# A fused retention and hard-swish MoE kernel: seven input buffers instead of six, and other places for transposes and attention steps between the matmuls

## The chip, the core and the metric

The kernel runs on one core of one Trainium2 chip. A core has five engines with a queue of instructions each: TensorE (PE: matmuls; PEld is its weight load), VectorE (DVE), ScalarE (ACT), GpSimd (POOL) and SyncE (SP), and 16 DMA engines that all queues share. The metric is the device time of one execution in microseconds (us), as the median of several runs. A profile is one further execution with a trace.

## What is computed

Retention (attention with a decaying causal mask and no softmax) for 8 batches and 8 heads, 576 positions, head size 64; its output, put together over the heads, goes through two matrix products with a hard-swish between them:

```python
scores = scale * np.matmul(q, k.transpose(0, 1, 3, 2))
ret = scores * Dmat[None, :, :, :]        # gamma[h] ** (i - j) for i >= j, else 0
attn = np.matmul(ret, v)
x = attn.transpose(0, 2, 1, 3).reshape(4608, 512)
h = x @ w_in                              # 512 -> 2048
g = h * np.clip(h + 3.0, 0.0, 6.0) / 6.0
out = g @ w_out                           # 2048 -> 512
```

## The kernel before

**Pieces.** The sequence of each batch is cut into four main pieces of 128 positions and a rest of 64; two rests make one "rest" piece. That gives 36 pieces, numbered 0 to 35 in the order of work; 12, 21, 30 and 35 are rest pieces. Within a batch a state (the decayed sum of k times v) is carried from one main piece to the next; a rest piece ends a batch and updates no state.

**Blocks.** The 4,608 tokens form nine blocks of 512: block b has the four main pieces of batch b, block 8 all the rests. For each block GEMM1 (`g1`, L539, 16 groups of four matmuls, then a Relu on ACT at L546 and a gate `gt` on DVE at L547) is followed by GEMM2 (`g2`, L597, 16 units of four matmuls: four token groups with four parts each; the last part copies the output to SBUF at L601 and stores it from SP at L582). GEMM1 of a block needs the outputs `xt16` of its four pieces.

**What lies between the matmuls.** Attention of later pieces is put between the units of GEMM2, by a list written by hand: `steps_at[block][j]` names what comes behind unit j (-1: ahead of the first), and `put` (L782 on) runs it. A step ends one pair of pieces and begins the next: `step` for pairs 8/9 and 10/11, `step4` from pair 12/13 on. `step4` multiplies the ended pair's queries with the carried state (L444), makes the scores of the begun pair (L411) and its state updates (L497), then the ended pair's attention times v (L465) and its copies to `xt16`. On DVE it does the state sums (L513, L528, L529) and the mask (L417). A tiny copy on ACT (`seen`, L456) reads the end of the first products, and the ended pair's last matmuls wait for it.

**What a piece needs ahead of its step.** `load` (L85) issues three DMAs from POOL (kn, q and v; six half-size ones for a rest piece), which also convert to 16 bit. `ahead` issues a DMA transpose of k from SP (`transpose_k`, L289), a scaling of q and v on DVE (`transpose_q`, L294), and a DMA transpose of the scaled q from SP (L295). `ahead_at[block][j]` says behind which unit. Pieces 0 to 7 are transposed on PE instead.

**Queues and buffers.** Every queue works in order, so that an instruction that waits holds what is behind it. Loaded pieces lie in `NBUF` = 6 buffers of kn and of qv. A buffer is taken by a later piece when its state update has read kn, its k is transposed, and its q and v are scaled; `load_until` only sets the place in the program, and as POOL issues nothing but these loads in this part, it is the waits that set their time. A buffer that is given back first is taken first. `step4` calls `load_until` for its last begun piece plus NBUF.

**Holds.** A manual dependency keeps loads 12 and later back until q of piece 10 is scaled (`transpose_q_and_load`, L701).

**Places that the change touches:** `NBUF` (L83), `update_mm` (L346 on), `first_step` (L669 on), `transpose_q_and_load`, and the tables from L826 on.

Of the kernel before, what the change touches and what calls it, by code (L numbers as in the profile page):

```python
# [17 lines left out]
def kernel(  # L18
# [16 lines left out]
    nc = tc.nc  # L35
# [4 lines left out]
    NPAIR = H // 2  # L40
# [14 lines left out]
    for b in range(B):  # L55
# [3 lines left out]
        if b >= 2 and b % 2 == 0 or b == B - 1:  # L59
            j = (b - 1) // 2  # L60
# [19 lines left out]

    loaded = {}
    EARLY = 4
    NBUF = 6  # L83

    def load(c):  # L85
        kn = nat.tile([P, H, D], FP16, tag="kn", bufs=NBUF, name=f"kn_{c}")
        qv = nat.tile([P, 2, H, D], FP16, tag="qv", bufs=NBUF, name=f"qv_{c}")
        loaded[c] = {"kn": kn, "qv": qv, "q16": qv[:, 0], "dma": []}
        for dst, src in ((kn, k), (qv[:, 0], q), (qv[:, 1], v)):
            for p0, b, s0, n in pieces[c][3]:  # L90
                loaded[c]["dma"].append(nc.gpsimd.dma_start(  # L91
                    dst[p0:p0 + n], src[b, :, s0:s0 + n, :].rearrange("h s d -> s h d")))
# [22 lines left out]
    first = const.tile([P, 1], FP32)  # L115
# [81 lines left out]
    def run_later(n):  # L197
        for _ in range(n):
            if later:
                later.pop(0)()  # L200
# [128 lines left out]
    def intra(c, copy_later=False, more=False):  # L329
        o, at, vs = st[c]["o"], st[c]["at"], st[c]["vs"]  # L330
        for p in range(NPAIR):
            for h2 in range(2):
                r = slice(h2 * HALF, h2 * HALF + HALF)
                nc.tensor.matmul(o[r, p, :], vs[:, 2 * p + h2, :], at[:, h2, p, :],  # L334
                                 start=(st[c]["first"] and p == 0),
                                 stop=(p == NPAIR - 1 and not more), skip_group_check=True)
        g0 = column_of(c)

        def copy():
            nc.scalar.copy(xt16[:, :, g0:g0 + P], o)  # L340

        if copy_later:
            return copy
        copy()

    def update_mm(cs):  # L346

        if not cs:
            return
        u = psum.tile([P, len(cs), NPAIR, D], FP32, tag="tu", name=f"u_{cs[0]}")  # L350
        for j, c in enumerate(cs):
            kn, vs = loaded[c]["kn"], st[c]["vs"]
            st[c]["u"] = u[:, j]
            for p in range(NPAIR):
                for h2 in range(2):
                    r = slice(h2 * HALF, h2 * HALF + HALF)
                    nc.tensor.matmul(u[r, j, p, :], kn[:, 2 * p + h2, :], vs[:, 2 * p + h2, :],
                                     start=(j == 0 and p == 0),
                                     stop=(j == len(cs) - 1 and p == NPAIR - 1),
                                     skip_group_check=True)  # L360

    def update_state(c, copies_later=False):
        kind, b, i, _ = pieces[c]
        last = i == PER - 1
        u = st[c]["u"]
        scale = gc_b[1 if i == PER - 1 and b % 2 else 0]
        ts = work.tile([P, NPAIR, D], FP16, tag="te" if last else "ts", bufs=4, name=f"ts_{c}")
        if i == 0:
            nc.vector.tensor_tensor(out=ts, in0=u, in1=scale, op=ALU.mult)
        else:  # L370
            ta = work.tile([P, NPAIR, D], FP32, tag="ta", bufs=2, name=f"ta_{c}")
            nc.vector.tensor_tensor(out=ta, in0=u, in1=st[c - 1]["ts"], op=ALU.add)
            nc.vector.tensor_tensor(out=ts, in0=ta, in1=scale, op=ALU.mult)
        st[c]["ts"] = ts
        old = state_of.get(b)
        if last:

            state_of[b] = None
            ts_of[b] = lambda h2, p: ts[rows(h2), p, :]
        else:  # L380
            new = free_tbd.pop(0)
            state_of[b] = new
        if old is not None and st[c].get("o") is not None:
            free_tbd.append(old)
        elif old is not None:
            st[c]["before"] = old
            st[c]["last_reader"] = True

        def copies():
            nc.scalar.copy(tbd[new][0:HALF, :, 0:D], ts[0:HALF])  # L390
            nc.scalar.copy(tbd[new][HALF:P, :, D:2 * D], ts[HALF:P])

        if last:
            return
        if copies_later:
            later.append(copies)
        else:
            copies()
# [192 lines left out]
    def g2(kb, mc, part):  # L591
        gt = gts[kb]
        if part == 0:
            pouts[kb, mc] = psum.tile([P, DM], FP32, tag="ph", bufs=4, name=f"pout_{kb}_{mc}")
        pout = pouts[kb, mc]
        for fc in range(4 * part, 4 * part + 4):
            nc.tensor.matmul(pout, gt[:, fc, P * mc:P * mc + P], wout16[:, fc, :],  # L597
                             start=(fc == 0), stop=(fc == NFC - 1))
        if part == 3:
            osb = work.tile([P, DM], FP32, tag="osb", bufs=4, name=f"osb_{kb}_{mc}")  # L600
            nc.scalar.copy(osb, pout)  # L601
            store(kb, mc, slice(0, DM), osb)
# [55 lines left out]
    def load_until(c):  # L658
        while next_load[0] < NP and next_load[0] <= c:
            load(next_load[0])  # L660
            next_load[0] += 1
# [4 lines left out]
    def unit2(kb, mc, part):  # L666
        return lambda: g2(kb, mc, part)

    def first_step(c):  # L669


        old, new, b = c - 1 >= EARLY, c + 1 < 8, pieces[c - 1][1]
        if old:
            before = state_of.get(b)
            tag, bufs = ("ph", 4) if c == 6 else ("o", 1)
            o = psum.tile([P, NPAIR, P], FP32, tag=tag, bufs=bufs, name=f"o_{c - 1}")
            st[c - 1].update(o=o, first=True)
            copy = intra(c - 1, copy_later=True, more=before is not None)
            update_mm([c - 1])
            load_until(min(c - 1 + NBUF, 11))  # L680
            update_state(c - 1, copies_later=True)
        if new:
            q_by_pe(c + 1)
        if old and new:
            run_later(9)
        if EARLY <= c < 8:
            scores(c, 0)
        if old and before is not None:
            for p in range(NPAIR):
                nc.tensor.matmul(o[:, p, :], tbd[before][:, p, :], st[c - 1]["qk"][:, 0, p, :],  # L690
                                 start=False, stop=(p == NPAIR - 1), skip_group_check=True)
        if new:
            k_by_pe(c + 1, "ph" if old else "tu")
        if old:
            copy()
        if c < 8:
            run_later(9)
        if EARLY <= c < 8:
            scale_v(c)

    def transpose_q_and_load(c):  # L701

        scaled = transpose_q(c)
        load_until(7 + NBUF)
        tc.add_manual_dep(
            loaded[12]["dma"][0].ins, scaled.ins.name,
            mybir.DependencyInfo(mybir.DependencyClass.Sync, mybir.DependencyReason.DATA),
            reason="transposes of block 2 first")

    def ahead(c):  # L710
        transpose_k(c)
# [22 lines left out]
    def step(ended, begun):  # L734
# [10 lines left out]
        for c in begun:  # L745
            load_until(c + NBUF)
            run_later(1)
# [5 lines left out]
    def step4(ended, begun):  # L753
# [5 lines left out]
        if ended:  # L759
            inter_done(ended)  # L760
            intra4(ended)
            outputs4(ended)
        load_until(begun[-1] + NBUF)
        for c in begun[:-1]:
# [52 lines left out]
    for fc, cols in ((2, done), (0, last), (1, last), (3, done), (2, last), (3, last)):  # L817
# [7 lines left out]

    pairs = [[c, c + 1] for c in range(8, NP, 2)]  # L826
    steps_at = {1: {-1: [(step, [], pairs[0])], 7: [(step, pairs[0], pairs[1])],
                    12: [(step, pairs[1], [])], 15: [(load_until, 18)]},
                2: {-1: [(step4, [], pairs[2])]}}
    i = 2  # L830
    for kb, at in ((2, (4, 8, 13)), (3, (4, 12)), (4, (4, 12)), (5, (4, 12)), (6, (2, 6))):
        for j in at:
            steps_at.setdefault(kb, {})[j] = [(step4, pairs[i], pairs[i + 1])]
            i += 1
    steps_at[6][10] = [(inter4, pairs[i]), (inter_done, pairs[i])]
    steps_at[6][11] = [(end4, pairs[i])]

    ahead_at = {1: {10: 12, 11: 13, 13: 14, 14: 15, 15: 16}, 2: {0: 17, 2: 18, 7: 19, 14: 20, 15: 21},
                3: {0: 22, 1: 23, 13: 24, 14: 25}, 4: {0: 26, 1: 27, 13: 28, 14: 29},
                5: {0: 30, 1: 31, 12: 32, 13: 33, 14: 34, 15: 35}}  # L840
    for kb in range(1, NMB - 1):
        steps = steps_at.get(kb, {})
        for j, c in ahead_at.get(kb, {}).items():
            steps.setdefault(j, []).append((ahead, c))
        put([unit2(kb, mc, part) for mc in range(MBLK // P) for part in range(4)], steps)
        gts.pop(kb)
        gemm1(kb + 1, {})
# [34 lines left out]
```

## Time and profile before

| What | Value |
|---|---|
| Median of 3 runs | 310.26 us (310.15 to 310.31) |
| Profiled execution | 311.19 us |
| Its span, first to last instruction | 309.4 us |
| Mean granted TensorE clock | 0.989 |
| GEMM1 matmuls, L539 (128x512) | 560 in the trace, 123.3 us busy |
| GEMM2 matmuls, L597 (128x512) | 560 in the trace, 127.5 us busy |
| Scalings of q and v, L294 | 28, mean 685 ns |
| Gates, L547 | 144, mean 687 ns |
| DMA transposes of k and of q, to landing | 28 each, median 4.5 and 4.6 us |
| Loads of kn, q, v (128 KB), to landing | 32 each, median 5.6, 5.6 and 6.8 us |

Busy time of an engine is the union of its instructions. Waits are put down to the event that ended last before the waiting instruction began. The time outside the span is 311.19 - 309.4 = 1.8 us. "Landing" runs from the start of a DMA's issue to its completion. In the timelines each row begins with its start and its length in us, and brackets hold the idle time of the engine before it and what ended it.

### The profile page before, as it was taken

Reading aid. Unit: us, or ns where it says so; the run is one execution under the profiler, and the core shown is the slowest. Engines: PE = TensorE matmul, PEld = TensorE weight load, DVE = VectorE, ACT = ScalarE, POOL = GpSimd, SP = SyncE. Lnnn points to the kernel's source line nnn. Section 1 sums busy time; section 2 is a strip of 40 time slices with the busy share of each in tenths; the row PEclk is TensorE's granted clock in tenths of the full one; section 3 lists DMA queues with packets and bytes.
Section 4 is the critical chain, followed back from the end, with each engine's and each line's share of the span. In section 5 each row is a group of like instructions: output and inputs, shape, how many; then the busy total and the mean of one; then the engine's idle time right before and its main releaser. Section 6 shows DMA issues by size and latency. Waiting matters only on the chain.

```text
span 309.4 us, 7338 instructions
## 1 busy us (share of the span) xinstructions
PE 296.9 (96%) x3035; PEld 148.0 (48%) x3035; DVE 179.2 (58%) x307; ACT 167.2 (54%) x302; POOL 107.7 (35%) x134
## 2 busy tenths in 40 slices
PE   6999999999999986999999999999999999999994
PEld 2654455545544543445544554455445544444443
DVE  4768437895768753775097519754886337207700
ACT  5468447764378342673367436743774457227611
POOL 8963587086900686333240275323000000000000
PEclk9999999999999996899999999999999999999999
DMA  9999999999997999999992999899330110010022
GB/s 70 151 201 202 190 157 210 159 142 152 182 194 110 91 179 170 150 115 75 168 137 69 53 188 142 108 95 171 68 90 15 57 70 0 34 70 34 1 68 68
DMA packets 153169, 35.60 MB, mean 115 GB/s; under 512 B 143792, under 2 KB 148656, under 8 KB 153136
## 3 DMA queue, kind: packets, MB, share of 16 engines
q0 software_dynamic: 117264, 18.36, 91.2%
q1 hardware_dynamic: 35472, 16.26, 29.4%
q8 instruction: 23, 0.38, 0.5%
q10 hardware_dynamic: 400, 0.52, 0.5%
q14 instruction: 10, 0.08, 0.1%
HBM read 36.70 MB, written 9.44 MB: 149 GB/s over the span
## 4 chain that ended last, share of the span: by engine, by line
PE 79%; DMA 8%; issue 6%; DVE 3%; POOL 2%; ACT 1%; POOLq 0%; DVEq 0%
PE ph L539 33%; PE pout L597 33%; DMA qk<-vs 3%; DMA qv<-in_q_dram 3%; DMA qk<-kn 2%; PE o L444 2%; PE ph L562 1%; POOL kn L91 1%; PE pout L610 1%; PE o L465 1%; PE o L334 1%; PE sc L305 1%; PE sc L411 1%; PE trq L227 1%; PE u L497 1%
## 5 line engine op out<-in xcount | busy, mean ns | idle before, releaser
L597 PE MATMUL pout<-wout,gt 128*128 128x512 f16 x560 | 127.5, 383 | 0.0
L547 DVE SCALAR_TENSOR_TENSOR gt<-u,ph 128x512 f16<-128x512 f32 x144 | 97.4, 687 | 47.5 <-ACT u L546 47.1
L539 PE MATMUL ph<-xt,win 128*128 128x512 f16 x560 | 123.3, 380 | 1.0 <-DVE gt L547 1.0
L546 ACT ACTIVATE u<-ph,cb 128x512 f32<-128x512 f32 x144 | 98.4, 687 | 26.8 <-PE ph L539 24.7
L539 PEld LDWEIGHTS <-win 128*128 128x128 f16 x560 | 54.9, 98 | 67.8 <-issue 2.9
L597 PEld LDWEIGHTS <-gt 128*128 128x128 f16 x560 | 53.5, 98 | 62.6 <-issue 1.6
L91 POOL DMA_DIRECT2D kn<-in_k_dram x40 | 34.6, 867 | 92.9 <-PE u L497 56.8
L601 ACT COPY osb<-pout 128x512 f32<-128x512 f32 x35 | 20.5, 586 | 58.8 <-PE pout L597 57.9
L91 POOL DMA_DIRECT2D qv<-in_q_dram x40 | 34.6, 870 | 4.5 <-DMA wout<-in_moe_w_out_dram 3.1
L91 POOL DMA_DIRECT2D qv<-in_v_dram x40 | 34.8, 877 | 2.0 <-DMA wout<-in_moe_w_out_dram 1.7
L294 DVE TENSOR_TENSOR vs<-qv,gqv 128x1024 f16<-128x1024 f16 x28 | 18.1, 685 | 2.0 <-DMA qv<-in_q_dram 2.0
L309 DVE TENSOR_TENSOR at<-sc,mask_wide 128x1024 f16<-128x1024 f32 x9 | 11.0, 1222 | 13.9 <-PE sc L305 13.8
L513 DVE TENSOR_TENSOR th<-u,ts 128x256 f32<-128x256 f32 x15 | 6.4, 425 | 21.1 <-PE u L497 20.7
L528 DVE TENSOR_TENSOR ta<-u,th 128x256 f32<-128x256 f32 x20 | 8.4, 420 | 15.9 <-ACT th L516 15.1
L417 DVE TENSOR_TENSOR at<-sc,mask 128x1024 f16<-128x1024 f32 x12 | 14.6, 1217 | 4.4 <-PE sc L411 4.4
L475 ACT CAST xt<-o 128x512 f16<-128x512 f32 x16 | 8.6, 589 | 9.6 <-PE o L465 9.6
L456 ACT COPY seen<-o 128x1 f32<-128x1 f32 x12 | 1.9, 160 | 15.9 <-PE o L444 15.9
L518 ACT CAST tm<-th 128x256 f16<-128x256 f32 x20 | 8.2, 412 | 2.5 <-DVE th L513 1.9
L411 PE MATMUL sc<-qk 64*64 64x64 f16 x384 | 6.3, 197 | 3.1 <-DMA qk<-vs 3.1
L529 DVE TENSOR_TENSOR ts<-ta,gc 128x256 f16<-128x256 f32 x20 | 8.5, 425 | 0.7
L340 ACT CAST xt<-o 128x512 f16<-128x512 f32 x11 | 6.3, 589 | 3.5 <-PE o L690 1.7
L219 ACT COPY qk<-trk 128x512 f16<-128x512 f16 x8 | 4.7, 587 | 4.9 <-PE trk L218 4.8
(89 smaller groups left out, 159.5 us busy)
## 6 DMA issues: line engine op xcount, KB each, us to landing
out_dram<-osb SPq DMA_DIRECT2D x32, 256.0 KB, 4.3
kn<-in_k_dram POOLq DMA_DIRECT2D x32, 128.0 KB, 5.6
qv<-in_q_dram POOLq DMA_DIRECT2D x32, 128.0 KB, 5.6
qv<-in_v_dram POOLq DMA_DIRECT2D x32, 128.0 KB, 6.8
wout<-in_moe_w_out_dram POOLq DMA_DIRECT2D x4, 512.0 KB, 15.2
win<-in_moe_w_in_dram POOLq DMA_DIRECT2D x3, 512.0 KB, 8.0
win<-in_moe_w_in_dram POOLq DMA_DIRECT2D x2, 256.0 KB, 5.6
kn<-in_k_dram POOLq DMA_DIRECT2D x8, 64.0 KB, 4.1
```

What stands on the lines that cost most here:

```text
L91: loaded[c]["dma"].append(nc.gpsimd.dma_start(dst[p0:p0 + n], src[b, :, s0:s0 + n, :].rearrange("h s d -> s h d")))
L294: scaled = nc.vector.tensor_tensor(out=vs, in0=loaded[c]["qv"], in1=gqv, op=ALU.mult)
L309: later.append(lambda: nc.vector.tensor_tensor(out=at.rearrange("t a b s -> t (a b) s"), in0=sc.rearrange("t a b s -> t (a b) s"), in1=mas ...
L411: nc.tensor.matmul(sc[rows(half), h2, j, p, :], qk[rows(h2), 1, p, rows(half)], qk[rows(h2), 0, p, rows(half)], start=True, stop=True)
L417: nc.vector.tensor_tensor(out=at.rearrange("t a j p s -> t (a j p) s"), in0=sc.rearrange("t a j p s -> t (a j p) s"), in1=mask64[:, None, ...
L475: nc.scalar.copy(xt16[:, :, g0:g0 + 2 * P].rearrange("e p (j x s) -> e p j x s", j=2, x=2) [:, :, :, half, :], o[half].rearrange("e j p s ...
L529: nc.vector.tensor_tensor(out=ts, in0=ta, in1=scale, op=ALU.mult)
L539: nc.tensor.matmul(ph, win16[:, dmc, P * fc:P * fc + P], xt16[:, dmc, t0:t0 + MBLK], start=(dmc == 0), stop=(dmc == NCC - 1))
L546: nc.scalar.activation(u, ph, ACTF.Relu, bias=cb[:, 0:1], scale=1.0 / 6.0)
L547: nc.vector.scalar_tensor_tensor(out=gts[kb][:, fc, :], in0=u, scalar=1.0, in1=ph, op0=ALU.min, op1=ALU.mult)
L597: nc.tensor.matmul(pout, gt[:, fc, P * mc:P * mc + P], wout16[:, fc, :], start=(fc == 0), stop=(fc == NFC - 1))
L601: nc.scalar.copy(osb, pout)
```

## The change

`NBUF` becomes 7. `update_mm` returns its last matmul, and the manual dependency gets a helper, `hold`: loads 10 and 11 are held to the state updates of pieces 4 and 5, load 12 to the scaling of piece 10.

```diff
-    NBUF = 6
+    NBUF = 7
...
+    def hold(c, after):
+        tc.add_manual_dep(
+            loaded[c]["dma"][0].ins, after.ins.name,
+            mybir.DependencyInfo(mybir.DependencyClass.Sync, mybir.DependencyReason.DATA),
+            reason="what is wanted sooner has the queues")
...
-            update_mm([c - 1])
-            load_until(min(c - 1 + NBUF, 11))
+            added = update_mm([c - 1])
+            load_until(min(c + 5, 11))
+            if c + 5 in (10, 11):
+                hold(c + 5, added)
...
-        load_until(7 + NBUF)
-        tc.add_manual_dep(
-            loaded[12]["dma"][0].ins, scaled.ins.name,
-            mybir.DependencyInfo(mybir.DependencyClass.Sync, mybir.DependencyReason.DATA),
-            reason="transposes of block 2 first")
+        load_until(13)
+        hold(12, scaled)
```

The tables get other places. Steps in GEMM2 of block 2 stand behind units 3, 7 and 12 instead of 4, 8 and 13; in blocks 3 to 5 the second step stands behind unit 11 instead of 12; in block 6 the second step and the end of the last pair move two units back.

```diff
-                    12: [(step, pairs[1], [])], 15: [(load_until, 18)]},
+                    12: [(step, pairs[1], [])]},
...
-    for kb, at in ((2, (4, 8, 13)), (3, (4, 12)), (4, (4, 12)), (5, (4, 12)), (6, (2, 6))):
+    for kb, at in ((2, (3, 7, 12)), (3, (4, 11)), (4, (4, 11)), (5, (4, 11)), (6, (2, 8))):
...
-    steps_at[6][10] = [(inter4, pairs[i]), (inter_done, pairs[i])]
-    steps_at[6][11] = [(end4, pairs[i])]
-
-    ahead_at = {1: {10: 12, 11: 13, 13: 14, 14: 15, 15: 16}, 2: {0: 17, 2: 18, 7: 19, 14: 20, 15: 21},
-                3: {0: 22, 1: 23, 13: 24, 14: 25}, 4: {0: 26, 1: 27, 13: 28, 14: 29},
-                5: {0: 30, 1: 31, 12: 32, 13: 33, 14: 34, 15: 35}}
+    steps_at[6][12] = [(inter4, pairs[i]), (inter_done, pairs[i])]
+    steps_at[6][13] = [(end4, pairs[i])]
+
+    ahead_at = {1: {10: (12,), 11: (13,), 13: (14,), 14: (15,), 15: (16, 17)},
+                2: {1: (18,), 3: (19,), 9: (20,), 10: (21,)}, 3: {0: (22,), 1: (23,), 7: (24,), 8: (25,)},
+                4: {0: (26,), 1: (27,), 7: (28,), 8: (29,)}, 5: {0: (30,), 1: (31,), 7: (32,), 8: (33,)},
+                6: {0: (34,), 1: (35,)}}
```

`ahead` of a piece that stands behind the same unit as a step comes after that step. With these lists the scaling and the transposes of 17 move ahead of GEMM1 of block 2, those of 18 to 21 to earlier units of block 2, those of 24, 25, 28, 29, 32 and 33 from the end of a GEMM2 to its middle, and those of 34 and 35 into block 6.

## The prediction

> **What bounds the kernel now.** I read the page first, then the waits of PE, its timeline around the one visible hole, the chain back from there, and last the queues behind it.
>
> ```profile
> PE 296.9 (96%) x3035; PEld 148.0 (48%) x3035; DVE 179.2 (58%) x307; ACT 167.2 (54%) x302; POOL 107.7 (35%) x134
> PEclk9999999999999996899999999999999999999999
> ```
>
> PE is busy for 96% of the span, so it sets the time; only its holes, and the slices with a lower clock, can be won. The clock digit falls at slices 15 and 16 (116 to 131 us), and nowhere else.
>
> ```profile
> PE sc L411 <- DMA qk<-vs: 3.1, 1, 3.1
> ...
> PE ph L539 <- DVE gt L547: 1.0, 2, 0.6
> PE o L444 <- issue: 0.8, 1, 0.8
> ```
>
> These three are all of PE's waits after 51 us. The columns are total us, times, longest. The first and third are one place:
>
> ```profile
> 114.98 0.19 PE L444 MATMUL o<-qk,ts 64*64 64x64 f16 x1
> 115.98 0.28 PE L444 MATMUL o<-qk,ts 64*64 64x64 f16 x7 [0.81 <-issue]
> ...
> 116.21 0.31 PE L411 MATMUL sc<-qk 64*64 64x64 f16 x14
> 119.58 0.43 PE L411 MATMUL sc<-qk 64*64 64x64 f16 x16 [3.06 <-DMA qk<-vs]
> ```
>
> This is the attention step that begins pieces 18 and 19, inside GEMM2 of block 2. The scores of 19 wait for its transposed q. The stretch after the wait runs at half clock (columns: PE, PEld, DVE, ACT, POOL busy, granted clock, DMA, GB/s):
>
> ```profile
> 118.50:125.40 6.90, 5.83 (x91) 2.79 (x91) 4.66 (x9) 2.37 (x5) 4.40 (x6) 0.51 2.18 172
> ```
>
> Why the transposed q is late, from the chain, then SP's and POOL's queues:
>
> ```profile
> 110.87 8.67 DMA qk<-vs
> ```
> ```profile
> 103.02 1.19 SPq L295 DMA_TRANSPOSE qk<-vs  x1
> 104.32 1.21 SPq L289 DMA_TRANSPOSE qk<-kn  x1
> ...
> 109.09 1.68 SPq L289 DMA_TRANSPOSE qk<-kn  x1
> 110.87 1.72 SPq L295 DMA_TRANSPOSE qk<-vs  x1
> ```
> ```profile
> 82.45 0.93 POOL L91 DMA_DIRECT2D kn<-in_k_dram  x1
> ...
> 99.91 0.88 POOL L91 DMA_DIRECT2D kn<-in_k_dram  x1 [14.78 <-PE u L497]
> ...
> 105.18 0.88 POOL L91 DMA_DIRECT2D kn<-in_k_dram  x1 [2.64 <-PE u L497]
> ```
>
> The transposition of q19 is issued at 110.87 and takes 8.67 us to land, where the page's median for this kind is 4.6. It is issued late because its scaling on DVE stands at 108.85, and lands late because loads 20 and 21 (issued 105.18 to 111.9) are in the same DMA engines. POOL idles 14.78 us before load 19 (99.91): six buffers, and the next becomes free only with the state update of piece 13.
>
> The DVE wait of PE is at 159.68 and 191.04. Before the first:
>
> ```profile
> 157.75 1.29 DVE L294 TENSOR_TENSOR vs<-qv,gqv 128x1024 f16<-128x1024 f16 x2
> 158.95 3.20 DVE L547 SCALAR_TENSOR_TENSOR gt<-u,ph 128x512 f16<-128x512 f32 x5
> ```
>
> Two scalings of 0.64 us stand behind the step's state work and ahead of GEMM1's first gates; five gates then run without a gap, PE having filled its banks.
>
> **The change, part by part.** No instruction is added or removed; order and waits move.
>
> *Seven buffers.* Loads to 15 keep their times: 10 and 11 are held by the same updates as now, 12 by the same scaling, and POOL does not idle at 14. Load 16 need not wait for update 10 (POOL's 2.60 us idle at 77.25): it goes at 74.6; 17 and 18 at 77.25 and 79.85. Load 19 takes the buffer of 12, a rest piece that has no state update, and asks only for 12's transposition, which load 18 already meets at 82.45. So 19 is issued at 82.45, not 99.91, and 20 at 99.91, not 105.18.
>
> *Transposes sooner, steps one unit earlier.* A unit of GEMM2 is four matmuls, 4.42/5 = 0.88 us (99.46 to 103.88 holds five). The new walk: 99.46 + 4 x 0.88 = 103.00, step 14/15 (103.88 to 105.24: 1.36) to 104.36, four units (3.56) to 107.92, step 16/17 (108.80 to 110.41: 1.61) to 109.53, five units to 113.95, step 18/19 (as these two, 1.5) to 115.45, three units to 118.10. GEMM1 of block 3 then begins at 118.10, now at 124.18: 6.08 us. It takes 14.41 us now (to 138.59) against 13.90 for the one of block 2 (85.05 to 98.95): 0.51 more. Together 6.6. Cross-check: holes 0.81 + 3.06, and half of 119.58 to 125.40 (2.91), are 6.8. I take 6.6.
>
> *Is q19 there in time?* Step 18/19 wants it some 0.65 us in, at 114.6. Its scaling follows the DVE work of step 14/15, which ends 0.88 earlier than now (108.92): scaled at 108.7, issued then. With the median 4.6 it lands at 113.3, with today's 8.67 at 117.4: 0 to 2.8 us of hole. Which? By work: up to its landing at 119.54 the engines now also carry load 19 (3 x 0.87, POOL's spacing), two transposes (of 17 and 18; 1.30 each, SP's spacing at 103.02 and 104.32) and a store (estimate 1.4, what is left of 99.91 to 119.54 after nine loads and five transposes, with some 2.5 us of start), 6.6 us that move away; 1 to 1.5 of it does not fit into the lull of 95 to 101 us and stays. 119.54 - 6.6 + 1.2 = 114.1: in time by 0.5. I take 0.2.
>
> The row says that a transposition waits out the loads issued ahead of it. The Trainium skill ("DMA: Bandwidth & Descriptors", section on queues, rings and completion order) says that each DMA engine goes round between the queues packet by packet; by that q19 would share from its issue and land near 113, and the 0.2 would fall away. Landing 8.67 against 4.6 speaks for the row.
>
> *Scaling of 17 moves ahead of GEMM1 of block 2.* DVE works in order: behind it stand that GEMM1's gates, and PE waits for these when four banks are full (fifth group at 85.05 + 4 x 0.864 = 88.5). Now the scaling of 16 ends a 1.98 us wait at 84.47, for a v issued at 78.99: 5.5 us. Load 17 has that slot, with three loads (2.6) more in front: it lands at 84.5 to 87.1. From 87.1, scaling and first gate (0.69 each) end at 88.5. 0 to 0.1 us; up to 0.9 if 17 gains nothing. I take 0.2.
>
> *Scalings of 20 and 21* go in front of step 18/19's state work, wanted at about 115.3. Load 21 goes 104.3 to 108.4; the page's medians of 4.7 (half loads) to 6.8 give 113.1 to 115.2, scaled by 115.9 at worst. State work (120.46 to 124.32: 3.9) ends by 119.8; the first gate is wanted at 118.10 + 1.84 = 119.9. Nothing, with 1.6 us of banks behind it.
>
> *Later blocks:* second step behind unit 11, scalings at units 7 and 8. The state work of 182.88's step ends 6.3 us after its start, the first gate is wanted at 1.7 + 4 x 0.88 + 1.84 = 7.0. The 1.0 us of PE's DVE waits goes. The copy of unit 11's output (0.59) now stands on ACT ahead of the small copy that releases the step's last matmuls; it ends some 0.8 us into the step, they begin at 0.9: nothing, or 0.1 in each of five steps without that cover. On SP the stores stand behind more transposes; four output buffers cover that. Transposes 22/23 to 30/31 keep some 2.5 us to their steps (now 3.4). In block 6 the last step ends two units before GEMM1 of block 7 instead of four; its two copies (0.37 + 0.39) end 0.9 us ahead of it: nothing.
>
> **Sum.** 6.6 + 1.0 - 0.2 - 0.2 = 7.2. Span 309.4 - 7.2 = 302.2; the profiled execution takes 311.19, 1.8 outside its span: 304.0. It is 0.93 above the median of the plain runs (310.26), so the median should read 303.1.
>
> **The rivals.**
>
> 1. *q19 is still late.* Landing 8.67 after its issue gives a hole of 2.8 us. For: the engines are full from 104 us on either way. Against: 6.6 us of work is gone from in front. The hole alone gives 310.26 - 7.6 + 2.8 = 305.5; with the half clock that set in 2.3 us after PE ran dry (116.2 to 118.5) and lasted 6.8, some 3.1 more: 308.6. The Trainium skill ("TensorE: Matmul & The Clock Gate", Part 1) puts the drop behind an idle window of 3.4 us that runs freely; by that a hole of 2.8 may go without it, and 305.5 would stand. The row dropped sooner.
>
> 2. *Load 19 doesn't move*, because its buffer is not free at 82.45. For: on POOL it stands behind every earlier load, and any of them that waits holds it. Against: load 18 meets the very same transposition today without idling. Then only the DVE waits go: 309.3.
>
> 3. *Slower: DVE held by piece 17.* One instruction, the scaling of 17, with all gates of GEMM1 of block 2 behind it. PE's hole is landing + 0.69 + 0.69 + 0.1 - 88.5 = landing - 87.0, and beyond 2.3 us the half clock adds about 2.9. It eats the 7.6 when 17 lands after 91.7, 4.6 us later than I expect. For: 70 to 80 us has the busiest DMA of the trace (2.8 of 5 us), and load 16 adds to it. Against: the v that is issued in this slot now lands by 84.47. A landing at 94 gives 310.26 - 7.6 + 7.0 + 2.9 = 312.6.
>
> **How the numbers follow.** No new hole, 302 to 304.3: 0.72. Rival 1, 304.3 to 308.6: 0.14. Rival 2: 0.05. Rival 3, slower: 0.09. The time is that of the first, 303.1. The range begins at 301.9: 310.26 - 7.6 with neither 0.2 taken is 302.7, the cross-check's 6.8 gives 302.5, and 0.6 is left for PE's small waits on issue ahead of weight loads (4.3 us in nine places at L444), of which a less crowded DMA may spare some. It ends at 306.5, in the midst of rival 1. A change within 0.2% (0.6 us) can't be told from none: faster 0.88, same 0.03, slower 0.09.
>
> **What would show it.** Right: clock 1.00 throughout after 51 us, no DMA wait of PE, POOL's load at 82 followed by one more without the 14.78 us idle, no scalings directly ahead of gates in blocks 3 and 4. Wrong: PE waiting at L411 (L412 in the new numbering) near 114 us (rival 1), a DVE wait for qv near 86 us with PE waiting for a gate at 88.5 (rival 3), or POOL idle to 99.9 before load 19 (rival 2).

## The result, and the profile after

| What | Before | After |
|---|---|---|
| Median of the runs side by side | 310.28 us (310.15 to 311.26) | 307.17 us (307.02 to 307.6) |
| Profiled execution | 311.19 us | 307.60 us |
| Its span | 309.4 us | 305.8 us |
| Mean granted TensorE clock | 0.989 | 0.987 |
| Loads of v, to landing | 6.8 us | 8.2 us |

The changed kernel takes 0.9895 of the time before (95% interval 0.9873 to 0.9918): 3.1 us less, where 7.2 were forecast, and 0.7 us above the end of the forecast range (306.5). Ratios, here and below, leave out executions that were over 1.5% longer than the fastest of their kernel, while medians and ranges hold all of them, so that a ratio isn't the quotient of two medians. What the change was to remove is gone; two other waits stand in its place. First the page of the changed kernel: PE's share, and the clock in 40 slices.

```profile
PE 294.1 (96%) x3035; PEld 146.6 (48%) x3035; DVE 179.7 (59%) x307; ACT 167.7 (55%) x302; POOL 107.9 (35%) x134
PEclk9599999999999999999999999999999999999999
```

The dip at slices 15 and 16 has gone; there is one at the start instead, where before had none. PE's waits after 60 us (total us, times, longest):

```profile
PE ph L540 <- DVE gt L548: 2.0, 1, 2.0
PE ph L540 <- issue: 1.0, 1, 1.0
PE sc L412 <- DMA qk<-vs: 0.2, 1, 0.2
```

The 3.1 us for the transposed q of 19 (L411, now L412) are 0.2, and the two gate waits of before (at 159.68 and 191.04) are gone. New are one gate wait of 2.0 and an "issue" of 1.0, at these places of PE's timeline:

```profile
85.65 3.62 PE L540 MATMUL ph<-xt,win 128*128 128x512 f16 x16
91.22 10.52 PE L540 MATMUL ph<-xt,win 128*128 128x512 f16 x48 [1.96 <-DVE gt L548]
...
117.55 0.32 PE L412 MATMUL sc<-qk 64*64 64x64 f16 x16 [0.17 <-DMA qk<-vs]
...
120.97 2.11 PE L540 MATMUL ph<-xt,win 128*128 128x512 f16 x9
124.09 2.12 PE L540 MATMUL ph<-xt,win 128*128 128x512 f16 x9 [1.01 <-issue]
```

GEMM1 of block 2 begins at 85.65, runs its first 16 matmuls (four banks of four) and stops for the first gate. The reader sees why in DVE's timeline:

```profile
85.02 0.69 DVE L294 TENSOR_TENSOR vs<-qv,gqv 128x1024 f16<-128x1024 f16 x1 [1.93 <-issue]
89.88 0.69 DVE L294 TENSOR_TENSOR vs<-qv,gqv 128x1024 f16<-128x1024 f16 x1 [4.17 <-DMA qv<-in_v_dram]
90.49 0.68 DVE L548 SCALAR_TENSOR_TENSOR gt<-u,ph 128x512 f16<-128x512 f32 x1
```

DVE waited 4.17 us for the v of piece 17, with the gates behind that scaling. POOL issued this load at 79.60; it took 10.2 us to land (the row of that one issue: operation, count, KB, us to landing).

```profile
qv<-in_v_dram POOLq DMA_DIRECT2D x1, 128.0 KB, 10.2
```

This is the sign that the prediction named for rival 3. The signs that it named for being right came out too, but for the 0.17 us of DMA wait: the clock is 1.00 from 14.7 us to the end of the work, in the chain of waits the transposition of q19 is now sent at 111.49, and in POOL's queue load 19 (85.22) comes ahead of the 14.78 us of idle time, and load 20 behind it:

```profile
111.49 6.02 DMA qk<-vs
```
```profile
85.22 0.88 POOL L91 DMA_DIRECT2D kn<-in_k_dram  x1 [1.65 <-DMA qv<-in_v_dram]
...
102.63 0.88 POOL L91 DMA_DIRECT2D kn<-in_k_dram  x1 [14.78 <-DMA qk<-vs]
```

Laid beside the prediction's walk, the profiled execution is 3.6 us longer than forecast (307.6 against 304.0):

| Stretch | Forecast | Profile after | Difference |
|---|---|---|---|
| Start of GEMM1 of block 2 | 85.05 (as before) | 85.65 | +0.6 |
| GEMM1 of block 2 | 14.41 + 0.2 | 16.53 | +1.9 |
| GEMM2 of block 2 | 118.10 - 99.46 + 0.2 = 18.84 | 18.79 | 0 |
| GEMM1 of block 3 | 13.90 | 15.00 | +1.1 |
| From there to the end | 170.78 - 1.0 = 169.8 | 169.81 | 0 |

The first row lies ahead of what the change moves: 0.5 us of it is there at the very first GEMM1 (19.15 against 18.63). From 7.9 to 14.7 us this execution ran at a clock of 0.50, the one of before at 1.00, but that this dip is the cause isn't shown: E4's profile has no dip and begins GEMM1 of block 2 at 85.69, E6's has one of 3.4 us and begins it at 84.46. Over the profiles below the start ranges from 84.46 to 86.23 us. The other two rows are the gate wait and the "issue" hole.

### The profile page after: what moved, and what is told of

Same layout as the page of the kernel before. It is cut to its first block, busy times and chain, and to the rows that moved or that the text cites. A ratio compares the mean times of both kernels' runs of the same rounds, so it can differ in the third digit from the quotient of the medians.

```text
span 305.8 us, 7337 instructions
## 1 busy us (share of the span) xinstructions
PE 294.1 (96%) x3035; PEld 146.6 (48%) x3035; DVE 179.7 (59%) x307; ACT 167.7 (55%) x302; POOL 107.9 (35%) x134
## 4 chain that ended last, share of the span: by engine, by line
PE 80%; DMA 10%; POOL 3%; DVE 3%; issue 1%; ACT 1%; POOLq 0%; DVEq 0%; ACTq 0%
PE ph L540 35%; PE pout L598 34%; DMA qv<-in_v_dram 5%; DMA qv<-in_q_dram 3%; DMA qk<-vs 2%; PE o L445 2%; POOL qv L91 2%; POOL kn L91 1%; DVE gt L548 1%; PE o L466 1%; PE sc L412 1%; PE pout L611 1%; PE u L498 1%; PE trq L227 1%; PE ph L563 1%
## 5 line engine op out<-in xcount | busy, mean ns | idle before, releaser
L598 PE MATMUL pout<-wout,gt 128*128 128x512 f16 x560 | 125.8, 379 | 0.0
L529 DVE TENSOR_TENSOR ta<-u,th 128x256 f32<-128x256 f32 x20 | 8.4, 421 | 12.0 <-ACT th L517 11.2
L483 ACT CAST xt<-o 128x256 f16<-128x256 f32 x16 | 4.8, 386 | 3.9 <-PE o L466 3.9
L233 ACT CAST qk<-trq 128x512 f16<-128x512 f32 x7 | 4.1, 587 | 4.9 <-PE trq L227 4.8
```

The lines of the kernel that those rows point to most:

```text
L529: nc.vector.tensor_tensor(out=ta, in0=st[c]["u"][1], in1=st[c]["sum"], op=ALU.add)
```

## The experiments

Medians with the range of the runs; each ratio is to the kernel before on the same chip. Three chips were used: E1, E2, E5 and E6 share one, E3, E4, E7 and E8 another, E9 to E11 a third. The kernel before read 310.18, 310.47 and 310.48 us on them, its single runs from 308.3 to 312.2. "Holes" are PE's idle stretches after 60 us.

### Which part of the change gives what: E2, E4, E3

**E2**: the seven buffers and the holds of the change with the tables of before.

```diff
-    NBUF = 6
+    NBUF = 7
...
+            if c + 5 in (10, 11):
+                hold(c + 5, added)
```

> Seven buffers and the new holds, with all the places of steps and transposes as before the change. Theory (load 19 out of the way is the most of it): q of 19 is issued near 111 as now, lands near 117 instead of 119.5, and step 18/19, wanting it at 115.5, waits some 1.5 us with no half clock behind it; the 1.0 us of gate waits in blocks 3 and 4 stays: 310.3 - 6.6 + 1.5 = 305.2, below the changed kernel. Rival (the places are the most of it): q of 19 still lands at 119.5 and the time stays at 309 to 310.3.

310.94 us (309.7 to 311.78), ratio 1.0032 (1.0012 to 1.0052): nothing gained, rather a little lost. PE's waits of it:

```profile
PE sc L412 <- DMA qk<-vs: 3.6, 1, 3.6
PE ph L540 <- DVE gt L548: 1.0, 2, 0.6
```

Both waits of before are there, and the theory's 305.2 fell. The buffer lets load 19 go early (85.53), but loads 20 to 22 move up behind it: load 20 goes at 100.48, where before had 19 at 99.91. The transposition of q19, still sent at its old place (110.97), lands at 119.63, and before it landed at 119.54: the expectation had 117.

**E4**: the kernel before with the new tables of blocks 3 to 6 alone.

```diff
-    for kb, at in ((2, (4, 8, 13)), (3, (4, 12)), (4, (4, 12)), (5, (4, 12)), (6, (2, 6))):
+    for kb, at in ((2, (4, 8, 13)), (3, (4, 11)), (4, (4, 11)), (5, (4, 11)), (6, (2, 8))):
...
-                3: {0: 22, 1: 23, 13: 24, 14: 25}, 4: {0: 26, 1: 27, 13: 28, 14: 29},
+                3: {0: (22,), 1: (23,), 7: (24,), 8: (25,)},
+                4: {0: (26,), 1: (27,), 7: (28,), 8: (29,)}, 5: {0: (30,), 1: (31,), 7: (32,), 8: (33,)},
```

> The kernel before with the new places in blocks 3 to 6 alone (second step behind unit 11, no scaling behind it; block 6 as in the change). The prediction's term: PE's gate waits of 0.57 and 0.42 go, nothing new comes: 1.0 below before, 309.2. Rival (the output copy ahead of the small copy on ACT, or tighter transposes, give it back): 310.2.

308.76 us (308.24 to 309.92), ratio 0.9968 (0.995 to 0.9985): 1.7 us less by the medians, 1.0 by the ratio. Its profile shows 1.0, the two gate waits that have gone; block 2 keeps its holes.

```profile
PE sc L411 <- DMA qk<-vs: 2.6, 1, 2.6
PE o L444 <- issue: 0.5, 1, 0.5
```

**E3**: the changed kernel with `NBUF = 6`.

> The changed kernel with six buffers instead of seven. If buffers and places only work together: load 19 goes near 100 to 102 and its transposed q lands near 116, for 1.5 us of waiting; load 17 goes near 80 and lands at 90 or later, so the gates of GEMM1 of block 2 are held for 2 to 4 us: 307.5 to 310. Rival (the places alone do it, the seventh buffer gives only the crowding): 306 or less.

308.33 us (307.29 to 311.42), ratio 0.9947 (0.9911 to 0.9982). The new tables without the buffer keep half of the gain by this ratio, and nearly all of it beside the 0.994 that the changed kernel reads in E9. But there are four holes in its profile; those for the gate and for q19 (L412) are longer than in the changed kernel, and the one at L529 is new. The last is of the same kind as the gate wait: DVE waited 4.47 us for a v ahead of a scaling at 122.47, and the state sums (L529 among them) stood behind it.

```profile
PE ph L540 <- DVE gt L548: 2.8, 1, 2.8
PE ph L540 <- DVE ta L529: 0.6, 1, 0.6
PE sc L412 <- DMA qk<-vs: 0.6, 1, 0.6
PE o L445 <- issue: 0.3, 1, 0.3
```

So the places do most of the work. Buffer and holds alone give nothing; what the buffer is worth with the places stays open (308.33 here, 307.17 and, in E9, 308.63 for the change, on three chips, with intervals that overlap).

### The gate wait of piece 17: E1, E5, E6

**E1**: 17 goes back to its place of before, behind the first unit of GEMM2 of block 2.

```diff
-    ahead_at = {1: {10: (12,), 11: (13,), 13: (14,), 14: (15,), 15: (16, 17)},
-                2: {1: (18,), 3: (19,), 9: (20,), 10: (21,)}, 3: {0: (22,), 1: (23,), 7: (24,), 8: (25,)},
+    ahead_at = {1: {10: (12,), 11: (13,), 13: (14,), 14: (15,), 15: (16,)},
+                2: {0: (17,), 1: (18,), 3: (19,), 9: (20,), 10: (21,)}, 3: {0: (22,), 1: (23,), 7: (24,), 8: (25,)},
```

> The changed kernel, but the transposes and the scaling of piece 17 stand behind unit 0 of block 2's GEMM2 again, instead of ahead of GEMM1 of block 2. Theory (the scaling of 17 holds the gates): PE's 1.96 us wait for a gate in GEMM1 of block 2 goes, and the time falls by 1.8 to 2.1 from 307.2, to about 305.2. Rival (the hole only moves): two more transposes (2.6 us) then stand on SP between 103 and 106 us ahead of those of 18 and 19, and the scores of 19 wait 1 to 2.5 us: 306 to 307.5.

307.83 us (305.47 to 310.22), ratio 0.9914 (0.9887 to 0.9941). The gate wait is gone, and one for q19 has come in its place, as the rival has it, though the time is a little above the rival's 306 to 307.5:

```profile
117.25 0.32 PE L412 MATMUL sc<-qk 64*64 64x64 f16 x16 [2.19 <-DMA qk<-vs]
```

**E5**: the changed kernel, but SP holds the transposition of the scaled q of 12, and so all that SP issues behind it, until the v of 17 has landed.

```diff
-        nc.sync.dma_start_transpose(st[c]["qk"][:, 0], vs[:, 0].rearrange("s h d -> s (h d)"))
+        t = nc.sync.dma_start_transpose(st[c]["qk"][:, 0], vs[:, 0].rearrange("s h d -> s (h d)"))
+        if c == 12:
+            tc.add_manual_dep(
+                t.ins, loaded[17]["dma"][2].ins.name,
...
```

> The changed kernel with one wait more: SP's transposition of the scaled q of 12, and with it all that is behind it on SP (12 to 17, one store), waits until v of 17 has landed. If the DMA engines share their turns between the queues (what SP issues after v17 delays it), v17 lands near 87 instead of 89.8 and PE's wait for a gate falls from 1.96 us to 0.4 or less: near 305.7, if no later transposition is missed. If they serve in the order of issue, v17 lands at 89.8 as it did, the wait stays at 2.0, and the time at 307 or more.

309.09 us (308.28 to 310.17), ratio 0.9963 (0.9941 to 0.9985). In DVE's timeline the scaling of 17 now starts at 87.64, for a load issued at 78.79: it landed after at most 8.85 us, against 10.2. This is one profile; but the same load took 9.85 to 12.30 us in all eight other profiles with seven buffers whose trace has its landing, so that 8.85 is the shortest by 1.0.

```profile
87.64 0.69 DVE L294 TENSOR_TENSOR vs<-qv,gqv 128x1024 f16<-128x1024 f16 x1 [2.07 <-DMA qv<-in_v_dram]
```

PE's gate wait fell from 1.96 to 0.53 us. Landing and wait are near what the theory of shared turns gave (87 and 0.4), so that the load did wait for work that was issued behind it. The changed kernel's own rows agree: SP issued that transposition at 81.31, 1.7 us after the load, and it landed 6.7 us later, at 88.0, ahead of the load's 89.8.

```profile
81.31 1.19 SPq L295 DMA_TRANSPOSE qk<-vs  x1
```
```profile
qk<-vs SPq DMA_TRANSPOSE x1, 6.7
```

The time isn't the theory's 305.7: it is lost again further on, in three "issue" holes (line numbers of this kernel are five higher):

```profile
PE o L450 <- issue: 1.5, 1, 1.5
PE ph L545 <- issue: 1.4, 1, 1.4
PE sc L417 <- issue: 0.9, 1, 0.9
```

**E6**: 17 is scaled inside GEMM1 of block 2, behind its unit 7, with eight of its gates ahead.

```diff
-        gemm1(kb + 1, {})
+        gemm1(kb + 1, {7: [(ahead, 17)]} if kb == 1 else {})
```

> The changed kernel with scaling and transposes of 17 behind the eighth group of GEMM1 of block 2 (by then v17 has landed). Theory (the scaling of 17 holds the gates only because v17 is not there): no wait for a gate over 0.1 us, since the banks cover one scaling of 0.69; transposes of 17 and 18 still go ahead of 103 us: 305.1. Rival (any scaling between gates costs its 0.69): 305.8.

306.25 us (306.0 to 308.87), ratio 0.9897 (0.9854 to 0.994). No gate wait and no wait for q19, and yet 1.1 us more than the theory's 305.1. Its profiled execution, the longest of its four, has 5.2 us of "issue":

```profile
109.33 0.44 PE L412 MATMUL sc<-qk 64*64 64x64 f16 x31 [1.16 <-issue]
...
114.84 0.26 PE L445 MATMUL o<-qk,ts 64*64 64x64 f16 x5
116.89 0.22 PE L445 MATMUL o<-qk,ts 64*64 64x64 f16 x3 [1.80 <-issue]
...
120.78 2.11 PE L540 MATMUL ph<-xt,win 128*128 128x512 f16 x9
125.11 2.12 PE L540 MATMUL ph<-xt,win 128*128 128x512 f16 x9 [2.23 <-issue]
```

### What "issue" is: E7, E8, E11

These holes break off in the midst of like matmuls: after 33 of step 16/17, after 13 of step 18/19, after nine of GEMM1 of block 3. The hole of the changed kernel at 124.09 is also behind nine matmuls of that GEMM1. Counted over PE and PEld, E6's three stand at instructions 1,977, 2,233 and 2,488, that is 255 or 256 apart, and the 0.81 us of before at 115.98 at 2,233 as well. In all thirteen profiles, every "issue" hole of PE over 0.15 us between 60 and 130 us stands at one of these three counts, give or take one. And the page of every kernel has a DMA queue that none of its lines issues to (packets, MB, share; 23 packets in some):

```profile
q8 instruction: 24, 0.39, 0.6%
```

That is 16 KB a packet, and 6,070 PE instructions over 24 packets are 253 each. The theory: PE's instructions come in blocks of 256, one DMA packet each; the next block is asked for when PE enters one, and that packet goes through the same DMA engines as the loads. A step is 120 or 128 matmuls with as many weight loads, about a whole block, gone in 1.5 us. In the changed kernel PE entered a block at 116.91. For the next 4.4 us the DMA engines were full (4,155 packets, 176 GB/s), and none of those was of this queue; its packet began at 121.38, took 1.36, and PE went on 1.35 us after its end, at 124.09. The queues from 116.95 to 121.30:

```profile
DMA packets 4155, 0.76 MB, mean 176 GB/s; under 512 B 4066, under 2 KB 4066, under 8 KB 4155
...
q0 software_dynamic: 3448, 0.44, 193.4%
q1 hardware_dynamic: 707, 0.33, 38.3%
```

**E7**: E6, with loads 22 and later held to the state updates of 18 and 19, so that fewer loads lie in the engines from 109 to 117 us. In E6 load 22 was issued at 107.86, here at 117.03.

```diff
-        update4(begun)
+        added = update4(begun)
...
-        load_until(begun[-1] + NBUF)
+        load_until(21 if begun[-1] < 19 else begun[-1] + NBUF)
+        if begun[-1] == 19:
+            hold(22, added)
```

> As the run with 17 inside GEMM1 of block 2, and loads 22 and later held until the last state update of step 18/19. Theory (PE's waits on issue are its instruction blocks, fetched late through the DMA engines that these loads fill): the waits on issue at the block boundaries (1.2, 1.8 and 2.2 us in the run without the hold) fall to 0.5 in all or less, the scores of 19 do not wait: 302.5 to 303.5, where the prediction was. Rival (the fetch is late for another reason, such as the density of small matmuls alone): 2 us or more of waits on issue stay, 305 or more.

304.89 us (304.77 to 305.57), ratio 0.9848 (0.9821 to 0.9875): below the medians of both kernels, though above the 302.5 to 303.5 expected. From the entry into a block to the start of the next packet it took 1.9 to 3.4 us ahead of the three places, where E6 had 3.9 to 5.4. One wait is left:

```profile
PE o L445 <- issue: 0.2, 1, 0.2
```

**E8**: the same hold in the changed kernel, with 17 still ahead of the gates.

> The changed kernel with loads 22 and later held until the last state update of step 18/19, 17 ahead of the gates as in the change. Theory: the gate wait of 2.0 us in GEMM1 of block 2 stays, since loads 22 and later come after it; the wait on issue (1.0) and that for the q of 19 (0.2) go: 306.0. Rival (the hold changes nothing): 307.2.

309.35 us (307.54 to 312.26), ratio 0.9962 (0.9926 to 0.9998). The theory gave 306.0. The "issue" hole is gone here too, but v of 17 landed at 90.19 in this execution, and the gate wait is longer, with half the clock behind it:

```profile
84.53 3.62 PE L542 MATMUL ph<-xt,win 128*128 128x512 f16 x16
91.61 12.21 PE L542 MATMUL ph<-xt,win 128*128 128x512 f16 x48 [3.47 <-DVE gt L550]
```

The same in windows of 3.41 us (us, PE, PEld, DVE, ACT, POOL busy, granted clock, DMA, GB/s):

```profile
88.66:92.07 3.41, 0.46 (x3) 0.22 (x3) 1.80 (x3) 0.41 (x1) 0.00 (x0) 1.00 1.75 156
92.07:95.48 3.41, 3.41 (x10) 1.17 (x9) 1.97 (x4) 1.63 (x3) 0.00 (x0) 0.50 1.76 156
```

**E11** puts the theory of blocks to a test that changes nothing near the holes: E6 with 21 more matmuls at the very start.

```diff
-    warm(7, MBLK)
+    warm(28, P)
```

> The version with 17 inside GEMM1 of block 2, loads untouched (it showed issue holes of 1.16, 1.80 and 2.23 us), with one edit: the seven warm-up matmuls of 512 columns at the start become 28 of 128 columns, the same columns in all. That puts 21 more matmuls ahead of everything. Theory (PE's instructions come in blocks of 128 matmuls with their 128 weight loads, and a hole stands where a block begins): every hole moves 21 matmuls ahead in the program. From the 34th matmul of step 16/17 to its 13th (the second group of L445), from the 22nd of step 18/19 to its first, and from the tenth matmul of GEMM1 of block 3 into the last three units of GEMM2 of block 2 (L598), its first matmul but one. Time 305 to 308 us. Rival (the holes belong to what PE does there, a step's first products or a GEMM1's start): they stay at the 34th, the 22nd and the tenth.

312.12 us (310.59 to 313.25), ratio 1.0056 (1.0026 to 1.0085). The expectation miscounts one place: in E6 the hole of step 18/19 is ahead of its 14th matmul, not its 22nd, so that 21 earlier is the eighth matmul before the step. There it is, and the other one is ahead of the twelfth matmul before GEMM1 of block 3, 21 before the tenth matmul of that GEMM1:

```profile
109.63 2.76 PE L598 MATMUL pout<-wout,gt 128*128 128x512 f16 x12
113.03 1.89 PE L598 MATMUL pout<-wout,gt 128*128 128x512 f16 x8 [0.63 <-issue]
...
115.76 0.67 PE L466 MATMUL o<-at,vs 64*64 64x64 f16 x32
121.25 4.89 PE L598 MATMUL pout<-wout,gt 128*128 128x512 f16 x12 [4.82 <-issue]
```

The first stands between two matmuls of GEMM2, the second between a step's last matmul and a unit of GEMM2. Counted over PE and PEld they are at the same places as in E6, 2,233 and 2,488, so that the rival (the holes belong to what PE does there) falls. The third hole, at step 16/17, has closed: that packet came in time. The time was forecast at 305 to 308 us and is 312.12. Between the two profiled executions (312.17, and 308.87 in E6) the "issue" holes grew from 5.2 to 6.0 us in sum, the last of these places from 2.23 to 4.82, and the clock was at 0.51 from 118.9 to 125.7, where E6 has 1.00. The block that PE entered at 113.03 now holds eight matmuls of GEMM2 and a whole step, 3.40 us of work; the next packet began 5.26 us after the entry, took 1.46, and PE went on 1.50 after that: 8.22 - 3.40 = 4.82.

### The changed kernel and E7 again: E9, E10

> The changed kernel once more, beside the best version and the kernel before on one chip. If piece 17's landing is what varies, its profile shows a gate wait of PE near 90 us somewhere between 0 and 3.5 us, and the time follows it: 306 to 309 us, 1.5 to 4 us below the kernel before. A third and further view of the late instruction block: an 'issue' hole, if there is one, stands in front of the tenth matmul of GEMM1 of block 3 (as at 124.09) or in front of the steps' matmuls at the same instructions as in the earlier profiles (the 34th matmul of step 16/17, the 22nd of step 18/19). Rival (holes fall anywhere): other instructions.

> Scaling of 17 inside GEMM1 of block 2, and loads 20 and 21 sooner with 22 held to the state updates of 18 and 19: the version that read 304.89 us. Theory (both of the changed kernel's losses are gone: no gate wait, nearly no late instruction block): 304.5 to 305.5 us, 1.5 to 3 us below the changed kernel on the same chip, PE's holes after 60 us below 0.5 us in sum. Rival (its 304.89 was the chip of that call): within 1 us of the changed kernel.

E9, the changed kernel: 308.63 us (306.96 to 312.81), ratio 0.994 (0.99 to 0.9981). E10, E7 once more: 305.22 us (304.72 to 306.05), ratio 0.9827 (0.9796 to 0.9858), with no hole over 0.15 us. On one chip the two are 3.4 us apart, a little more than the 1.5 to 3 expected. The single runs of the changed kernel spread over 5.9 us (4.2 without the longest), those of E10 over 1.3. E9's profile has a gate wait, this time 2.37 us, and no "issue" hole:

```profile
91.00 10.52 PE L540 MATMUL ph<-xt,win 128*128 128x512 f16 x48 [2.37 <-DVE gt L548]
```

So both of the changed kernel's waits differ from one execution to the next. (E10 was expected to have loads 20 and 21 sooner; they go at the same place as in the changed kernel, and only 22 and later move.)

## Why the prediction was right, and where it failed

**Direction and main term: right.** The 6.6 us of the step that begins 18 and 19 are all there. GEMM2 of block 2 took 18.79 us for a forecast of 18.84, the hole for q19 is 0.17 for a forecast of 0.2, and the half clock is gone. Corrected for the later start (GEMM2 began at 102.18 and not 99.46), q19 was to be sent at 111.4 and to land at 116.8; it went at 111.49 and landed at 117.51. Rival 1 (2.8 us of hole) did not come to pass in the changed kernel, though E1 shows how near it is: 2.19. That the landing of q19 came out so well is in part luck. The largest item of the work that was to move away, load 19 (3 x 0.87 of the 6.6 us), isn't borne out: in E2 load 19 is out of the way and q19 lands at 119.63 all the same, as loads 20 to 22 move up, and E3, with the new places and load 19 late (104.61), has a hole of 0.63 against 0.17. The two transposes of 17 fit better: with them back in front, q19 takes 7.67 us to land in E1, and 6.02 in the changed kernel.

**Buffers: right in kind.** POOL issued load 19 at 85.22 (82.45 was forecast) and then idled 14.78 us before load 20, so that rival 2 falls. E2 shows that the buffer alone is worth nothing.

**Later blocks: right.** 1.0 us forecast, 0.97 in the stretch from GEMM2 of block 3 to the end; E4 has it without the rest.

**"Scaling of 17 moves ahead of GEMM1 of block 2": this step failed.** It put the landing of load 17 at 84.5 to 87.1 and the cost at 0.2 us. The load landed at 89.80 and cost 1.96. It is rival 3's mechanism, short of the point from which that makes the kernel slower, and its formula for PE held: landing + 0.69 + 0.69 + 0.1 is 91.28, and PE went on at 91.22. What was wrong is the landing. Of the 2.7 us beyond 87.1, 0.6 is the later start of this execution; the other 2.1 is a landing of 10.2 us, where the prediction allowed 5.5 and 2.6 for three loads more in front.

The idea under it was that a place further ahead in POOL's queue lands that much sooner. In the eight profiles with seven buffers whose trace has its landing (E5 with its hold left out), this load was issued at 78.4 to 80.2 and landed at 89.0 to 90.7; in the three with six buffers it was issued at 81.6 to 82.2 and landed at 87.9 to 90.5. So going 1.4 to 3.8 us sooner did not land it sooner. E2, with the places of before, has 10.31 us too, so that the long landing comes with the loads that the seventh buffer lets go sooner, not with the new places.

The prediction also took it that a transfer waits out what is issued ahead of it. By that the landing would depend on three more loads in front; E5, which holds back the transposes and the store that SP issues later, has 1.35 us less (10.2 to at most 8.85). What made up the rest of the 2.1 wasn't settled. The Trainium skill ("DMA: Bandwidth & Descriptors", section on queues, rings and completion order) has each DMA engine go round between the queues packet by packet. The rows 81.31 and 79.60 agree with the skill; the prediction weighed this against one landing and took the other side.

**A term that the sum put at nothing:** 1.0 us, PE waiting for its own instructions. The row was in view (0.81 us of "issue" at 115.98 in the profile before) and was counted into the hole that would go. E7 and E11 show what it is.

**The clock behind a hole.** The prediction put the drop at holes "beyond 2.3 us". After 60 us, the four profiles with a longest hole of 1.96 to 2.37 (after, E1, E6, E9) kept the clock, and the six with one of 2.60 to 4.82 (E4, E3, before, E8, E2, E11) lost it, for 3.41 us or 6.83. The changes of the clock lie on a grid of 3.41 us, and the traces fit a rule on it rather than on the hole: in the grid's window right ahead of each of the six drops PE was idle for 2.35 (E3) to 2.96 us (E8), and in no window that kept the clock, while PE had work, for more than 1.79 (E9). The Trainium skill ("TensorE: Matmul & The Clock Gate", Part 1) has a window of 3.41 us that runs freely, and the lengths agree; but PE need not be idle for all of one, since 2.35 us was enough.

**From profile to median.** 0.93 us was taken off because the profiled execution of before lay that far above the median. After, it lies 0.43 above, in E7 0.12 below: this was scatter, not an offset. So the median was missed by 4.1 us: 3.6 by which the profiled execution was longer than the walk (0.6, 1.9 and 1.1), and 0.5 of this supposed offset. E7 has the forecast walk without the two losses. Its span is 303.0 against 302.2, of which 0.88 is the later start, and its medians are 304.89 and 305.22.

**A reading.** The "2.8 of 5 us" under rival 3 is the DMA column of the windows, a mean over the 16 engines that goes above 1 where packets overlap, not microseconds; nothing in the sum hangs on it.

## What to carry to other kernels

An instruction that waits for a DMA on an engine that others wait for belongs behind, or amid, what they need; the slack of a load is to be counted with everything that other queues issue until it lands, not only with what stands ahead of it, and where the DMA engines are full, a sooner issue may land no sooner. Dense stretches of small matmuls eat the instruction stream, and the next block of it comes through the same DMA engines as the loads: where "issue" holes come at equal counts of instructions, hold back the loads that aren't yet wanted.

## What the runs showed that was not expected

- PE's instructions arrive in packets of 16 KB, one for some 256 PE instructions. Counting on in 256s from the holes, after 140 us, in a quieter DMA, the packet began 0.7 to 1.9 us after PE entered a block at six places in ten; among the loads of 103 to 125 us it began up to 6.0 us after (E9). Where PE had run dry, it went on 1.3 to 1.9 us after the packet ended. By the same count a quarter of the packets after 140 us, and one of E8 at 123.99, began before PE reached the block, so that the count drifts or the request runs ahead of PE; when it is made isn't shown.
- The place of the block boundaries alone, moved by 21 warm-up matmuls, made a kernel 5.9 us longer (306.25 to 312.12 in the medians, on two chips; ratios 0.9897 and 1.0056 to before).
- The granted clock changes in steps of 3.41 us: the stretches at half are 3.41 or 6.83 us long, those between them whole multiples (105.81 is 31 of them).
- The same load of 128 KB, v of 17, took 6.3 to 8.5 us to land in three profiles with six buffers and 9.9 to 12.3 us in eight with seven.
